# Joining the value products of a head pair into five bursts instead of eight in an attention stage that TensorE shares with its transpositions

## The chip, the cores and the metric

The kernel runs on one core of a Trainium2 chip. The metric is the device time of one execution in microseconds, taken as the median of several runs. The engines are TensorE (PE, with its weight loads PEld), VectorE (DVE), ScalarE (ACT), GpSimd (POOL) and SyncE (SP, which issues DMAs). Each works through its own queue in order and waits on semaphores.

## The reference, cut to what matters

Attention with a mask by hash buckets, for 2 batches of 8 heads, 768 positions and 64 channels, and then two dense layers. The change touches the last line of the attention only, the product of the weights with the values.

```
scores = np.where(mask, scale * q @ k.T, -1e9)
attn = np.exp(scores - scores.max(-1))
attn = attn / (attn.sum(-1) + 1e-9)
out = attn @ v
x = moe(out); return moe2(x)
```

## The kernel before, in words

**Units and pairs.** The heads are taken in eight pairs, numbered here 0 to 7. A pair has 12 units: two heads (`e` 0 and 1) times six blocks of 128 query rows (`i` 0 to 5). A unit goes through four steps on three engines. `QK` on PE (L474, four products of 384 columns) fills a tile `sc` of scores. `MAX` on DVE (L482) reduces it, and `EXP` on ACT (L486) writes `P`. There are two `sc` tiles, so a `QK` waits until the `EXP` of the unit two before it has read its tile.

**Transpositions.** For each block of rows the `P` of both heads, 12 squares of 128x128, is transposed on PE in three pieces `T` of four squares (L509) into a PSUM bank `pt`. ACT copies the bank as the high half in 16 bits (`HI`, L518) and DVE writes the low half (`LO`, L521), both into a tile `PT`. There are two `pt` banks, which the small transpositions `R` of the row factors (L711) use too. So a `T` waits until the `LO` (or the copy of the `R`) two tiles before it has read its bank.

**Value products.** Two blocks of rows make a group of 256 columns, so a pair has three groups, 0 to 2. The products of a group with the values (`PV`, L566) are 36 matmuls of 64 weight columns into one bank `O`, two heads in turn into its lower and upper half. The generator `pv` cuts them into three parts of 12. `EV` on DVE (L575) scales the bank into `xr`. The group's factor comes from `R`, whose source `rb` POOL makes (L725).

**Other steps on PE.** For the next pair PE makes `z` (L398, hash bits) and `xp` (L407, the bits spread over the rows, two pairs of products with a bank of their own).

**The order.** A table `AT` gives each kind of step of a pair a due time, in units of which a pair has 12. Pair `q` adds 12 times `q`. All steps of all pairs are sorted by due time and recorded in that order, and each engine's queue follows from it. The nine due times of `PV` are three for each group. The second and third part of group 0 (9.95 and 10.07) have nothing of PE's between them, so a pair has eight separate bursts. After the attention the queue goes on with the dense layers, where PE is busy throughout.

Of the kernel before, what the change touches and what calls it, by code (L numbers as in the profile page):

```python
# [29 lines left out]
def lsh_attention_glu_act(ctx, tc, qt, kt, v, proj, w_gate, w_val, w_out1, w_in2, w_out2, ident_d, code_d, out):  # L30
# [309 lines left out]
    with ExitStack() as actx:  # L340
# [228 lines left out]
        def evac(b, p, g, O_ps):  # L569
            cs = slice(g * GN, (g + 1) * GN)  # L570
            if g == 0 and p % 2 == 0:
                XX[b, p // 2] = xtile(f"xr_{b}_{p}")
            if g == 0:
                X[b, p] = XX[b, p // 2][:, p % 2]
            nc.vector.scalar_tensor_tensor(out=X[b, p][:, cs], in0=O_ps[:, 0:GN], scalar=1.0 / PSCALE, in1=RS.pop((b, p, g)), op0=ALU.mult, op1=ALU.mult)  # L575
# [9 lines left out]
        with tc.manual_schedule():  # L585
# [109 lines left out]
            def at(kind, i, q, fn, *args):  # L695
                prog.append((UP * q + (AT[kind][i] if isinstance(kind, str) else kind), len(prog), fn, args))

            PP, NQ = {1: p1}, len(seq)
# [41 lines left out]
            for q in range(NQ):  # L740
                us = un[UP * q:UP * q + UP]
                for i, w in enumerate([us[m] for m in (1, 3, 0, 2)] + us[4:] if q == 0 else us):
                    at("QK", i, q, w.QK)
                    at("MAX", i, q, w.MAX)
                    at("EXP", i, q, w.EXP)
                for i in range(PCS * NI):
                    k = i if q else TO[i]
                    x = fl[NI * q + k // PCS]
                    at("T", i, q, x.T, k % PCS)
                    at("HI", i, q, x.HI, k % PCS)  # L750
                    at("LO", i, q, x.LO, k % PCS)
                for i in range(NI // GI):
                    w = us[2 * GI * i + 2 * GI - 1]
                    at((4.3, 7.35, 12.3)[i], 0, q, w.ST)
                    at("ST", i, q, w.ST2)
                    at("RB", i, q, RB, w)
                    at("R", i, q, R, w)
                    at("RS", i, q, RSC, w)
                    for s in range(3):
                        at("PV", 3 * i + s, q, PV, w, s)  # L760
                    at("EV", i, q, lambda w: evac(*w.O), w)
                b, p = seq[q]
                vs = [AT["VR"][0] - UP, AT["VT"][0] - UP, AT["V2"][0], AT["V3"][0], AT["V4"][0]]
                if q == 0:
                    vs[:2] = AT["MAX"][2] + 0.001, AT["MAX"][3] + 0.001
                    at(AT["QK"][3] + 0.001, 0, q, scale_out)
                    at(AT["T"][1] + 0.001, 0, q, scale_in)
                    at(AT["HI"][1] + 0.005, 0, q, scale_keep)
                    vs[2] = max(vs[2], vs[1] + 0.5)
                    vs[3] = max(vs[3], vs[2] + 0.1)  # L770
                    vs[4] = max(vs[4], vs[3] + 0.1)
                elif q == NQ - 1:
                    vs[2:] = (AT["RB"][2] - UP + 0.1 * i + 0.1 for i in range(3))
                for h, d in enumerate(vs):
                    at(d, 0, q, split_v, b, p, h)
                if q + 1 < NQ:
                    at(0.8, 0, q, load_v, *seq[q + 1])
                    if q:
                        at(min(AT["SCL"][0], AT["TOP"][0], AT["TOP"][1]) - 0.01, 0, q, prep, q + 1)
                        at("SCL", 0, q, on, q + 1, "scale")  # L780
                        for j in range(2):
                            at("TOP", j, q, on, q + 1, "top", j)
                            at("RST", j, q, on, q + 1, "rest", j)
                    for i in range(4):
                        at("Z", i, q, on, q + 1, "z", 3 * i, 3 * i + 3)
                        at("XP", i, q, on, q + 1, "xp", *divmod(i, 2))
                        at("H", i, q, on, q + 1, "H", *divmod(i, 2))
                    at("BITS", 0, q, on, q + 1, "bits")
                    at(AT["TOP"][0] + 0.001 if q else -0.9, 0, q, on, q + 1, "copy", 0, 0)
                    at(AT["TOP"][1] + 0.001 if q else -0.65, 0, q, on, q + 1, "copy", 1, 0)  # L790
                    for j in range(2):
                        for m in range(1, 3):
                            at(AT["Z"][3] + 0.01 * m + 0.001 * j, 0, q, on, q + 1, "copy", j, m)
                        at(AT["H"][2 * j + 1] + 0.03, 0, q, on, q + 1, "copy", j, 3)
                        at(AT["H"][3] + 0.035 + 0.005 * j, 0, q, on, q + 1, "copy", j, 4)
                        at(AT["TOP"][j] + 0.002 if q else AT["Z"][3] + 0.03, 0, q, on, q + 1, "copy", j, 5)
                    at(max(AT["H"][3], AT["Z"][3]) + 0.06, 0, q, on, q + 1, "done")
                if q + 2 < NQ:
                    at(0.9, 0, q, load_qk, *seq[q + 2])
            for i in range(12):  # L800
                q, t = ((1, 2.2), (1, 3.4), (1, 4.6), (2, 2.2), (2, 3.4), (2, 4.6), (2, 5.8), (3, 2.2), (3, 4.8), (4, 4.0), (4, 5.0), (4, 6.0))[i]
# [572 lines left out]
```

## Time and profile before

| | before |
|---|---|
| median of 3 runs | 787.75 us (786.75 to 788.44) |
| profiled execution, its own time | 789.26 us |
| span of its instructions | 787.4 us |
| mean granted TensorE clock | 0.997 of full speed |
| PE busy, share of the span | 98% |
| DVE, ACT, POOL busy | 79%, 66%, 21% |

The attention stage takes about the first 250 us. In a timeline row the first number is the start in us from the span's start, the second how long the merged instructions lasted from the first start to the last end, and `x8` how many were merged. The starts of matmuls are recorded. Their ends are modelled and reach beyond the start of the next one, so the distance from one start to the next is what a step occupies PE. Engine `PEld` rows are the weight loads, which run ahead of the products. What stands in square brackets is the idle time before the row, and what ended it.

### The profile page before, as it was taken

What the parts mean: (1) busy time and instruction counts of PE and PEld (TensorE: products, weight loads), DVE (VectorE), ACT (ScalarE), POOL (GpSimd) and SP (SyncE); (2) the same over time, 40 slices, a digit from 0 to 9 for tenths busy, and PEclk for the clock granted to TensorE, in tenths of its full rate; (3) what the DMA queues carried; (4) which work ended last, traced back from release to release, by engine and by line L of the source; (5) the groups of instructions that cost most, each with busy time, mean ns of one, the idle gap of its engine ahead of it and who ended that gap; (6) DMA issues with size and microseconds to landing.
All of it is one profiled execution on the core that took longest, in us unless ns stands there. A gap on an engine that the chain in (4) does not pass through costs nothing.

```text
span 787.4 us, 13055 instructions
## 1 busy us (share of the span) xinstructions
PE 771.5 (98%) x4912; PEld 702.6 (89%) x4912; DVE 624.9 (79%) x1095; ACT 523.1 (66%) x1027; POOL 165.4 (21%) x166
## 2 busy tenths in 40 slices
PE   8999999999989899999999999999999999999997
PEld 5778888888868899999999999999999998898986
DVE  6989988889976878778779959878988867666643
ACT  6988898888865564665664535446766667767653
POOL 4644686783595000000000000000000000000000
PEclk9999999999999999999999999999999999999999
DMA  8845456444101112213212431432333201000002
GB/s 234 198 124 154 100 172 164 105 118 109 34 1 55 54 55 87 75 54 91 72 53 83 133 107 59 147 116 85 104 108 107 82 0 64 18 1 1 0 1 81
DMA packets 41462, 66.98 MB, mean 85 GB/s; under 512 B 5630, under 2 KB 28542, under 8 KB 41398
## 3 DMA queue, kind: packets, MB, share of 16 engines
q1 hardware_dynamic: 40896, 65.82, 28.4%
q8 instruction: 39, 0.64, 0.3%
q10 hardware_dynamic: 502, 0.31, 0.1%
q14 instruction: 25, 0.20, 0.1%
HBM read 45.27 MB, written 3.15 MB: 61 GB/s over the span
## 4 chain that ended last, share of the span: by engine, by line
PE 66%; DVE 1%; ACT 0%; issue 0%; ACTq 0%
PE qa L298 3%; PE qa L296 3%; PE qa L297 3%; PE p L298 3%; PE p L296 3%; PE p L297 3%; PE y L296 2%; PE y L298 2%; PE y L297 2%; PE qe L296 2%; PE qe L298 2%; PE qe L297 2%; PE qb L296 2%; PE qb L298 2%; PE qb L297 2%; PE qa L1134 2%
## 5 line engine op out<-in xcount | busy, mean ns | idle before, releaser
L521 DVE SCALAR_TENSOR_TENSOR PT<-pt,PT 128x512 f16<-128x512 f32 x144 | 96.3, 684 | 16.6 <-ACT PT L518 13.6
L518 ACT ACTIVATE PT<-pt 128x512 f16<-128x512 f32 x144 | 82.4, 597 | 28.8 <-PE pt L509 28.4
L482 DVE TENSOR_REDUCE st<-sc 128x1 f32<-128x768 f32 x96 | 91.0, 949 | 5.3 <-PE sc L474 4.4
L486 ACT ACTIVATE P<-sc,st 128x768 f32<-128x768 f32 x96 | 86.9, 906 | 5.7 <-DVE st L482 5.3
L509 PE MATMUL pt<-ident,P 128*128 128x128 f32 x576 | 79.2, 275 | 2.8 <-DVE PT L521 1.9
L509 PEld LDWEIGHTS pt<-ident,P 128*128 128x128 f32 x576 | 66.1, 140 | 11.7 <-DVE PT L521 6.3
L566 PE MATMUL O<-PT,vh 128*64 128x256 f16 x576 | 54.9, 278 | 0.0
L298 PE MATMUL p<-yh,whl_i 128*128 128x384 f32 x128 | 42.9, 336 | 0.0
L296 PE MATMUL p<-yh,whl_i 128*128 128x384 f32 x128 | 42.9, 335 | 0.0
L297 PE MATMUL p<-yl,whl_i 128*128 128x384 f32 x128 | 42.9, 335 | 0.0
L566 PEld LDWEIGHTS <-vh 128*64 128x64 f16 x576 | 30.7, 109 | 11.2 <-issue 11.2
L1111 ACT ACTIVATE t<-p,cst 128x384 f32<-128x384 f32 x32 | 18.4, 574 | 27.2 <-PE p L298 27.2
L566 PE MATMUL O<-PT,vl 128*64 128x256 f16 x288 | 34.2, 273 | 0.1
L474 PE MATMUL sc<-H,H 128*128 128x384 f32 x96 | 29.6, 390 | 0.8 <-ACT P L486 0.8
L474 PE MATMUL sc<-N,N 128*128 128x384 f32 x96 | 28.9, 382 | 0.3 <-ACT N L412 0.3
L1116 DVE SCALAR_TENSOR_TENSOR gg<-p,t 128x384 f32<-128x384 f32 x32 | 17.7, 555 | 13.3 <-ACT t L1113 13.2
L261 ACT ACTIVATE qb<-qa 128x384 f32<-128x384 f32 x24 | 11.4, 475 | 25.2 <-PE qa L298 14.5
L261 ACT ACTIVATE qd<-qb 128x384 f32<-128x384 f32 x24 | 11.4, 475 | 23.6 <-PE qb L298 20.2
L389 POOL TENSOR_TENSOR W<-n,U 128x768 fp32r<-128x768 f32 x14 | 25.6, 1829 | 0.7
L474 PE MATMUL sc<-U,U 128*128 128x384 f32 x96 | 24.8, 339 | 0.0
L296 PEld LDWEIGHTS p<-yh,whl_i 128*128 128x128 f32 x128 | 24.0, 188 | 0.5
L297 PEld LDWEIGHTS p<-yl,whl_i 128*128 128x128 f32 x128 | 24.0, 188 | 0.5
(1220 smaller groups left out, 2537.0 us busy)
## 6 DMA issues: line engine op xcount, KB each, us to landing
wr_o<-in_moe_w_out_dram SPq DMA_DIRECT2D x28, 512.0 KB, 3.4
H<-U SPq DMA_DIRECT2D x29, 192.0 KB, 3.2
wr_i<-in_moe_w_in_dram SPq DMA_DIRECT2D x8, 512.0 KB, 3.6
wr_i<-in_moe_w_in_dram SPq DMA_DIRECT2D x16, 256.0 KB, 2.9
n<-in_qt_dram SPq DMA_DIRECT2D x8, 384.0 KB, 3.9
n<-in_kt_dram SPq DMA_DIRECT2D x8, 384.0 KB, 4.6
U<-W SPq DMA_DIRECT2D x16, 192.0 KB, 2.6
vr<-in_v_dram SPq DMA_DIRECT2D x8, 384.0 KB, 3.4
```

The lines of the kernel that those rows point to most:

```text
L261: nc.scalar.activation(out=self.new("bcd"[m]), in_=src, func=AF.Copy)
L296: nc.tensor.matmul(ps, lhsT=wh, rhs=rh, start=first, stop=False, **kw)
L297: nc.tensor.matmul(ps, lhsT=wh, rhs=rl, start=False, stop=False, **kw)
L298: nc.tensor.matmul(ps, lhsT=wl, rhs=rh, start=False, stop=last, **kw)
L389: nc.gpsimd.tensor_tensor(out=self.t4[j][1], in0=self.nat[j], in1=f(self.t4[j][0]), op=ALU.subtract)
L474: nc.tensor.matmul(self.sc[:, n, 0:HN], lhsT=M[:, ts], rhs=K[:, n * HN:(n + 1) * HN], start=s0, stop=not s0)
L482: nc.vector.tensor_reduce(out=self.st[:, 0, self.c:self.c + 1], in_=self.sc[:, :, 0:HN], op=ALU.max, axis=AX.XY, negate=True)
L486: nc.scalar.activation(out=self.P, in_=self.sc[:, :, 0:HN], func=AF.Exp, bias=self.st[:, 0, self.c:self.c + 1], scale=1.0, accum_out=self. ...
L509: nc.tensor.transpose(self.ps[m][:, j, :], un[2 * self.n + e].P[:, a, c:c + 128], ident)
L518: nc.scalar.activation(out=self.part(0, m), in_=self.ps[m], func=AF.Copy, scale=PSCALE)
L521: nc.vector.scalar_tensor_tensor(out=self.part(1, m), in0=self.ps[m], scalar=PSCALE, in1=self.part(0, m), op0=ALU.mult, op1=ALU.subtract)
L566: nc.tensor.matmul(O_ps[r, 0:GN], lhsT=vv[m][:, e, i * D:(i + 1) * D], rhs=PT[:, l, e * NI + i, :], start=(s == 0), stop=(s == len(steps) ...
```

## The change

The three parts of a group keep their order and their instructions. Only due times change, and only for pairs 0 to 6. For group 0 all three parts come at the time of the third, 10.07. For groups 1 and 2 the first part comes just ahead of the second, at 12.32 and 17.52. The third parts of these groups (15.54 and 19.68) stay. The last pair keeps its old times.

```diff
                     for s in range(3):
-                        at("PV", 3 * i + s, q, PV, w, s)
+                        k = 3 * i + s
+                        at(AT["PV"][k] if q == NQ - 1 or (i and s) else AT["PV"][3 * i + (2 if i == 0 else 1)] - 0.001 * (2 - s), 0, q, PV, w, s)
                     at("EV", i, q, lambda w: evac(*w.O), w)
```

with the table's row

```
"PV": (8.96, 9.95, 10.07, 11.73, 12.32, 15.54, 16.81, 17.52, 19.68),
```

On DVE, ACT, POOL and SP the same instructions stand in the same order as before. Only PE's queue differs. Group 0 in pair 3 stood on PE like this before. In the names `sc_3_1_4` is pair 3, head 1, block 4 (pairs 4 to 7 are called 0 to 3 again, since the batch's number is left out), `pt` is a transposition bank, `O_3_0` the products of group 0 of pair 3, and `...` stands for the rest of a part.

```order
L474 MATMUL sc_3_1_4_1773<-W_0_3_895,W_0_3_891 128x384 x2
L566 LDWEIGHTS vh_3_1719
L566 MATMUL O_3_0_1778<-PT_3_0_1528,vh_3_1719 64x256
...
L474 MATMUL sc_3_0_5_1813<-H_0_3_896,H_0_3_892 128x384 x2
L474 MATMUL sc_3_0_5_1813<-U_0_3_894,U_0_3_890 128x384 x2
L509 MATMUL pt_0_1819<-ident,P_3_0_4_1752 128x128 x4
L509 MATMUL pt_2_1830<-ident,P_3_1_3_1724 128x128 x4
L566 LDWEIGHTS vh_3_1719
L566 MATMUL O_3_0_1778<-PT_3_0_1528,vh_3_1719 64x256
...
L711 MATMUL r_3_1_3_1861<-ident,rb_3_1_3_1808 128x128 x2
```

The same place in PE's queue now:

```order
L474 MATMUL sc_3_1_4_1773<-W_0_3_882,W_0_3_878 128x384 x2
L474 MATMUL sc_3_0_5_1800<-H_0_3_883,H_0_3_879 128x384 x2
L474 MATMUL sc_3_0_5_1800<-U_0_3_881,U_0_3_877 128x384 x2
L509 MATMUL pt_0_1806<-ident,P_3_0_4_1752 128x128 x4
L509 MATMUL pt_2_1817<-ident,P_3_1_3_1724 128x128 x4
L566 LDWEIGHTS vh_3_1719
L566 MATMUL O_3_0_1824<-PT_3_0_1528,vh_3_1719 64x256
...
L711 MATMUL r_3_1_3_1861<-ident,rb_3_1_3_1795 128x128 x2
```

The first 12 products of the group moved behind one `QK` and two pieces `T`, and all 36 now stand in one row. In group 1 the first 12 move in the same way behind one `QK` of the next pair and two `T`.

Group 2 of pair 3 stood on PE like this before, from the piece `T` ahead of its first part (`sc_0_1_3` belongs to pair 4, `xp` to pair 5):

```order
L509 MATMUL pt_0_2090<-ident,P_0_0_2_2027 128x128 x4
L566 LDWEIGHTS vh_3_1719
L566 MATMUL O_3_2_2095<-PT_3_2_1824,vh_3_1719 64x256
...
L407 MATMUL xp_1_1_1_2113<-bt,code 128x384
L474 MATMUL sc_0_1_3_2118<-N_1_0_1340,N_1_0_1336 128x384 x2
L474 MATMUL sc_0_1_3_2118<-W_1_0_1338,W_1_0_1334 128x384 x2
L509 MATMUL pt_1_2123<-ident,P_0_0_2_2027 128x128 x2
L509 MATMUL pt_1_2123<-ident,P_0_1_2_2079 128x128 x2
L509 MATMUL pt_2_2133<-ident,P_0_1_1_2016 128x128 x4
```

and now:

```order
L509 MATMUL pt_0_2090<-ident,P_0_0_2_2027 128x128 x4
L407 LDWEIGHTS code
L407 MATMUL xp_1_1_1_2100<-bt,code 128x384
L474 MATMUL sc_0_1_3_2105<-N_1_0_1327,N_1_0_1323 128x384 x2
L474 MATMUL sc_0_1_3_2105<-W_1_0_1325,W_1_0_1321 128x384 x2
L509 MATMUL pt_1_2110<-ident,P_0_0_2_2027 128x128 x2
L509 MATMUL pt_1_2110<-ident,P_0_1_2_2079 128x128 x2
L509 MATMUL pt_2_2120<-ident,P_0_1_1_2016 128x128 x4
L566 LDWEIGHTS vh_3_1719
L566 MATMUL O_3_2_2125<-PT_3_2_1811,vh_3_1719 64x256
```

Here the first 12 moved behind one `xp`, one `QK` and two `T`.

## Rows read from the trace of the kernel before

**Rows 1.** Busy time by engine in one stretch: PE, PEld, DVE, ACT, POOL, clock, DMA.

```profile
100.00:140.00 40.00, 39.90 (x349) 33.77 (x349) 35.54 (x57) 35.47 (x75) 29.45 (x31) 1.00 0.58 160
```

**Rows 2.** Waits of PE's products from 20 to 230 us: total, times, longest.

```profile
PE pt L509 <- DVE PT L521: 1.7, 3, 1.1
PE r L711 <- POOL rb L725: 1.2, 1, 1.2
PE r L711 <- DVE PT L521: 0.4, 1, 0.4
PE xp L407 <- ACT bt L401: 0.4, 1, 0.4
```

**Rows 3.** Timeline of PE around group 0 of pair 3.

```profile
115.83 1.03 PE L509 MATMUL pt<-ident,P 128*128 128x128 f32 x8
116.62 0.60 PE L474 MATMUL sc<-N,N 128*128 128x384 f32 x2
...
117.50 0.30 PE L566 MATMUL O<-PT,vh 128*64 128x256 f16 x2
...
118.28 0.62 PE L474 MATMUL sc<-H,H 128*128 128x384 f32 x2
...
119.08 1.04 PE L509 MATMUL pt<-ident,P 128*128 128x128 f32 x8
120.05 0.30 PE L566 MATMUL O<-PT,vh 128*64 128x256 f16 x2
...
120.72 0.82 PE L566 MATMUL O<-PT,vh 128*64 128x256 f16 x12
121.48 0.44 PE L711 MATMUL r<-ident,rb 128*128 128x128 f32 x2
```

**Rows 4.** Timeline of ACT and DVE at the same place.

```profile
117.08 0.90 ACT L486 ACTIVATE P<-sc,st 128x768 f32<-128x768 f32 x1
...
118.60 0.69 DVE L521 SCALAR_TENSOR_TENSOR PT<-pt,PT 128x512 f16<-128x512 f32 x1
```

**Rows 5.** Timeline of PE and DVE around group 1 of pair 3.

```profile
122.45 1.04 PE L509 MATMUL pt<-ident,P 128*128 128x128 f32 x8
...
123.42 0.30 PE L566 MATMUL O<-PT,vh 128*64 128x256 f16 x2
...
123.74 1.29 DVE L521 SCALAR_TENSOR_TENSOR PT<-pt,PT 128x512 f16<-128x512 f32 x2
...
124.20 0.62 PE L474 MATMUL sc<-N,N 128*128 128x384 f32 x2
...
125.02 1.03 PE L509 MATMUL pt<-ident,P 128*128 128x128 f32 x8
```

**Rows 6.** Timeline at group 2 of pairs 2, 3 and 4: low halves and transpositions.

```profile
110.45 0.69 DVE L521 SCALAR_TENSOR_TENSOR PT<-pt,PT 128x512 f16<-128x512 f32 x1 [0.44 <-ACT PT L518]
111.20 0.33 PE L509 MATMUL pt<-ident,P 128*128 128x128 f32 x1
...
111.78 0.30 PE L566 MATMUL O<-PT,vh 128*64 128x256 f16 x2
...
138.27 0.66 DVE L521 SCALAR_TENSOR_TENSOR PT<-pt,PT 128x512 f16<-128x512 f32 x1
138.74 1.04 PE L509 MATMUL pt<-ident,P 128*128 128x128 f32 x8
...
166.16 0.66 DVE L521 SCALAR_TENSOR_TENSOR PT<-pt,PT 128x512 f16<-128x512 f32 x1
166.81 1.03 PE L509 MATMUL pt<-ident,P 128*128 128x128 f32 x8
```

**Rows 7.** Timeline at waits for others, in pair 0 and in pair 7.

```profile
40.85 0.27 DVE L540 TENSOR_REDUCE vrow<-vrow 1x1 f32<-1x129 f32 x1 [1.52 <-DMA vrow<-vm]
...
42.99 0.93 PE L509 MATMUL pt<-ident,P 128*128 128x128 f32 x5 [0.47 <-DVE PT L521]
...
226.86 0.44 PE L711 MATMUL r<-ident,rb 128*128 128x128 f32 x2 [1.21 <-POOL rb L725]
```

## The prediction

> **What bounds the kernel now.** I looked first at the busy time of each engine in a stretch of the attention stage. In 40 us PE is busy for 39.90, DVE for 35.54 and ACT for 35.47 [rows 1]. So PE sets the pace there, and the other two have only about a tenth of their time to spare. Next I read the waits of PE's products from 20 to 230 us: 1.7 + 1.2 + 0.4 + 0.4 = 3.7 us in all, six in number [rows 2]. PE practically never stands. A step that PE loses or gains in a pair therefore moves the end by the same amount, because the dense layers behind the attention are a PE stage too. Last I read the timeline around the three places that the change touches, once for PE, and once for the engines that give PE its tiles back. The reader should see there two things: what a burst costs PE beyond its products, and how long before each `QK` and each `T` its tile had come free.
>
> **What a burst costs.** From the start of two pieces `T` to the start of the `QK` right behind them PE takes 116.62 - 115.83 = 0.79 us [rows 3]. With 12 products between them it takes 124.20 - 122.45 = 1.75 [rows 5]. Inside a longer burst 12 products take 120.72 - 120.05 = 0.67 [rows 3]. So going into a burst and out of it costs 1.75 - 0.79 - 0.67 = 0.29 us. The change removes three bursts in each of seven pairs, 21 in all, which is 21 x 0.29 = 6.1 us of PE's time. That is what could be won. The row thus shows a price for changing between products of 128 and of 64 weight columns. The Trainium skill (TensorEngine Tiling (Array Packing), Key Properties) says why it may be there: changing the tiling mode, and not only the tile, drains TensorE. By that rule alone the change is a gain of these 6.1 us. The trace agrees that the price exists, but not that it is all that changes.
>
> **What the moved steps wait for.** In each of the three places 12 products now stand behind a `QK` and two `T` that they stood ahead of. PE comes to these three about 0.7 to 0.8 us earlier, so their tiles must be free that much earlier. I work it out by the last `T` of each place, since everything that PE does behind it is fixed: two `T` start 0.79 to 0.97 us ahead of what follows them [rows 3], so I put the second one at half of that, 0.44, behind the first. A `T` starts 0.06 us after the `LO` that frees its bank (110.45 + 0.69 = 111.14, and the `T` starts at 111.20) [rows 6]. A second `T` that has not waited is 0.53 ahead of the products (120.05 - 119.52), one that has waited 111.78 - 111.20 = 0.58 [rows 3, 6], so a wait costs 0.05 beside itself.
>
> *Group 0.* Before, the last `T` started at 119.08 + 0.44 = 119.52 [rows 3]. Its bank comes free with the `LO` that ends at 118.60 + 0.69 = 119.29 [rows 4], so it can't start before 119.35. The `QK` ahead of it waits too: PE would be ready for it at 116.62 + 0.80 = 117.42 (a `QK` takes 119.08 - 118.28), but the `EXP` that frees its tile ends at 117.08 + 0.90 = 117.98 [rows 3, 4]. The first products covered this wait, and this cover is gone. Neither the `EXP` nor the `LO` comes sooner in the new order: both work on tiles that PE filled ahead of the place, and their engines' queues are the same. So the `T` moves up by 0.17, and behind it stand 12 products more, 0.67. The end of the burst is late by 0.67 - 0.17 + 0.05 = 0.55 us. `R` at 121.48 comes at 122.03 [rows 3]. Seven pairs: 3.85 us.
>
> *Group 1.* The last `T` started at 125.02 + 0.44 = 125.46. The second of two `LO` ends at 123.74 + 1.29 = 125.03 [rows 5], so it can start at 125.09, 0.37 earlier. Late by 0.67 - 0.37 + 0.05 = 0.35. Seven pairs: 2.45 us.
>
> *Group 2.* Here the pairs differ [rows 6]. In pair 2 (and 1) the last `T` waited for its bank already, so it moves up by nothing: 0.67. In pair 3 (and 0) it started at 139.18 and the bank was free at 138.93: up by 0.19, late by 0.53. In pair 4 (and 5) it started at 167.25, the bank free at 166.82: up by 0.37, late by 0.35. Six pairs: 2 x (0.67 + 0.53 + 0.35) = 3.1 us. In pair 6 the place lies shortly ahead of the `R` at 226.86, for which PE waits 1.21 us on POOL's `rb` [rows 7]. A delay of 0.67 vanishes there: 0.
>
> **What is late next, and what takes a delay up.** Behind each burst PE's queue holds `R` or `xp` and the next `QK`, and for these wait `MAX` on DVE, `EXP` on ACT and then the next `T`. All of them shift by the same delay; PE can't catch up, since it had no waits to give away. The exceptions are waits on something that does not shift. In pair 0 DVE stands 1.52 us for a DMA at 40.85, and PE waits for the `LO` behind it at 42.99, 0.47 before that piece and a little more in the next [rows 7]. The delays of groups 0 and 1 of that pair go into it by some 0.6. The products need no other tile that is late: the bank `O` is evacuated ahead of a group's first part, which comes later now. Instructions that stay in place on the other engines cost nothing, as long as PE is the one that is waited for [rows 1].
>
> **Sum.** 3.85 + 2.45 + 3.1 - 0.6 = 8.8 us longer. The profiled execution's 789.26 becomes 798.1. It stands 1.5 above the median of the runs, so for that I predict 787.75 + 8.8 = **796.5 us**. As a check by PE's own account: idle time of about 2 us in a pair is added (0.6 ahead of the `QK` of group 0, the rest ahead of the `T`), some 15 in all, and 6.1 of switches saved, which leaves about 9.
>
> **The rivals.**
> *Faster: the switches are saved and nothing waits.* For it speaks the 0.29 us of a burst. It would give 787.75 - 6.1 = 781.7. It decides at the last `T`: where its bank is free 0.67 + 0.05 + 0.06 = 0.78 us ahead of its old start, nothing is lost, and with more something is won. The rows show 0.23, 0.43, 0.25, 0.43 and 0.06, so all three places are on the other side, and by 0.35 and more. Only a `LO` that comes much earlier in the new order would bring it, and nothing in the queues lets it. Chance 0.05. The rule of the Trainium skill on tiling modes would by itself give this time.
> *No change.* DVE and ACT, 89% busy, might be what really paces a pair, with PE's steps only filling in; then a lost or saved 0.5 us of PE would drown: 787.75. Against it, PE stands for only 0.1 us in 40 [rows 1]. Chance 0.03.
> *Half of it.* The rest of PE's waits, 3.7 - 0.6 = 3.1 us [rows 2], could take delays up as well, and group 2 could cost 0.35 in all six pairs (1.0 less): 8.8 - 3.1 - 1.0 = 4.7, which is 792.5. Chance 0.08.
> *More.* A burst of 36 products keeps PE for 121.48 - 120.05 + 0.67 = 2.1 us, in which ACT and DVE get no new tile. If they run dry, the `T` behind it come in a heap and wait, say, as long again as those of group 1 now do, 0.4 in each pair: 2.8 more, 799.3. Against it, both have queues that go on with earlier tiles in that time. Chance 0.04.
>
> **How the numbers follow.** The forecast with its own bounds has 0.80. It goes down to 793.4, if PE's other waits take up 3.1, and up to 798.7, if nothing is taken up (0.6 and 0.67 more) and group 2 costs 0.67 in all six pairs (2 x (0.14 + 0.32) = 0.9 more). To leave out no more than 2 in 10 the range takes in the nearer part of the half case: 793.0 to 798.7. A difference of 0.2%, 1.6 us, is about what this kernel's runs can tell from none. Faster 0.05, within it 0.03, slower 0.92, all from the cases above.
>
> **What would show it.** In the profile of the changed kernel PE's wait for `LO` ahead of `T` should be seen at two or three places of every pair, not three times in all, and a new wait of `QK` for `EXP` of about 0.6 us in each of seven pairs. PE's busy time from 100 to 140 us should fall from 39.90 to about 37.5. Products should stand in rows of 36, 24 and 12, with 0.67 for each 12. I am wrong if the `T` ahead of a joined burst start without waiting, or if a pair takes no longer though they wait. Then the `LO` would hang on PE's products in a way that the rows do not show.

## The result, and the profile after

The changed kernel takes 796.25 us (median of five runs, 795.24 to 798.22), the kernel before took 786.75 in the runs beside it. The ratio is 1.012, with a 95% interval of 1.0101 to 1.014, which is 7.9 to 11.0 us longer. The forecast was 8.8 us longer and 796.5 us in all. It counted from 787.75, 1.0 us above the median beside these runs, so part of the close agreement of the totals is luck.

PE's waits come first, since the prediction lives on them. These are the waits of PE's products in the changed kernel from 20 to 235 us: total, times, longest.

```profile
PE pt L509 <- DVE PT L521: 5.0, 14, 1.6
PE sc L474 <- ACT P L486: 4.2, 7, 0.9
PE r L711 <- POOL rb L725: 0.6, 1, 0.6
PE r L711 <- DVE PT L521: 0.4, 1, 0.4
PE xp L407 <- ACT bt L401: 0.3, 1, 0.3
PE xp L407 <- ACT N L412: 0.2, 1, 0.2
```

Before, `T` waited for `LO` three times and no `QK` for an `EXP` [rows 2]. Now it is 14 and 7 times, and the 7 are one in each changed pair. The sum has risen from 3.7 to 10.7 us. The busy time of the stretch that [rows 1] shows has changed with it:

```profile
100.00:140.00 40.00, 38.44 (x336) 32.85 (x333) 33.78 (x54) 33.00 (x69) 27.95 (x29) 1.00 0.57 160
```

PE has lost 1.5 us of its 40. DVE and ACT have lost 1.8 and 2.5, as the same 40 us now hold less of the work. (The view counts a product as busy to its modelled end, so the time from start to start has grown by more.)

Group 0 of pair 3 in the changed kernel, a timeline to lay beside [rows 3, 4]:

```profile
119.71 0.60 PE L474 MATMUL sc<-N,N 128*128 128x384 f32 x2
...
120.17 0.90 ACT L486 ACTIVATE P<-sc,st 128x768 f32<-128x768 f32 x1
...
120.97 0.19 ACT L486 ACTIVATION_READ_ACCUMULATOR P<-sc,st 128x1 f32 x1
...
121.22 0.62 PE L474 MATMUL sc<-H,H 128*128 128x384 f32 x2 [0.56 <-ACT P L486]
...
121.68 0.69 DVE L521 SCALAR_TENSOR_TENSOR PT<-pt,PT 128x512 f16<-128x512 f32 x1
122.04 1.05 PE L509 MATMUL pt<-ident,P 128*128 128x128 f32 x8
...
123.02 0.30 PE L566 MATMUL O<-PT,vh 128*64 128x256 f16 x2
...
124.35 0.82 PE L566 MATMUL O<-PT,vh 128*64 128x256 f16 x12
125.10 0.44 PE L711 MATMUL r<-ident,rb 128*128 128x128 f32 x2
```

The `QK` waits for the `EXP`, as foreseen, and to be exact for the readout of its sum, which ends at 121.16. From the `QK` before it to this one pass 121.22 - 119.71 = 1.51, where PE needs 0.80 for a `QK`. So the wait is 0.71 from start to start, of which the view shows 0.56. The second `T` starts at 122.04 + 0.44 = 122.48, and its bank was free at 121.68 + 0.69 = 122.37. So it did not wait for the `LO`; the `QK` had just held PE up long enough. The 36 products stand in one row, from 123.02 to 125.10, 2.08 us.

Group 1 of the same pair, to lay beside [rows 5]:

```profile
126.08 1.03 PE L509 MATMUL pt<-ident,P 128*128 128x128 f32 x8
...
126.90 0.61 PE L474 MATMUL sc<-N,N 128*128 128x384 f32 x2
...
127.36 1.29 DVE L521 SCALAR_TENSOR_TENSOR PT<-pt,PT 128x512 f16<-128x512 f32 x2
...
128.11 1.25 PE L509 MATMUL pt<-ident,P 128*128 128x128 f32 x8 [0.25 <-DVE PT L521]
...
128.71 0.42 PEld L509 LDWEIGHTS pt<-ident,P 128*128 128x128 f32 x4 [0.18 <-DVE PT L521]
```

Here the `QK` follows the two `T` at once, and both `T` behind it wait for their `LO`; the second for the one that ends at 127.36 + 1.29 = 128.65, and its weights follow at 128.71.

What each place costs is read best from the `R` of the three groups, which stand behind or between the places. Before, the `R` around 121.48 [rows 3] were

```profile
113.87 0.38 PE L711 MATMUL r<-ident,rb 128*128 128x128 f32 x2
...
130.19 0.41 PE L711 MATMUL r<-ident,rb 128*128 128x128 f32 x2
```

and in the changed kernel, around the one at 125.10,

```profile
116.95 0.38 PE L711 MATMUL r<-ident,rb 128*128 128x128 f32 x2
...
134.18 0.41 PE L711 MATMUL r<-ident,rb 128*128 128x128 f32 x2
```

The lag grows from 3.08 over 3.62 to 3.99: group 0 of pair 3 costs 0.54, group 1 costs 0.37. At the end of the attention stage the lag is 7.51 us, or 7.9 counted from the last `R` ahead of the first changed place (which stood 0.40 earlier in this execution). The runs' 9.5 has an interval from 7.9 to 11.0; what it may hold beyond the 7.9 of the attention is not shown by these two traces.

### The profile page after: what moved, and what is told of

It reads as the page before. It is cut to its first block, busy times and chain, and to the rows that moved or that the text cites. A ratio compares the mean times of both kernels' runs of the same rounds, so it can differ in the third digit from the quotient of the medians.

```text
span 793.5 us, 13055 instructions
## 1 busy us (share of the span) xinstructions
PE 770.6 (97%) x4912; PEld 702.4 (89%) x4912; DVE 625.9 (79%) x1095; ACT 524.7 (66%) x1027; POOL 165.2 (21%) x166
## 4 chain that ended last, share of the span: by engine, by line
PE 65%; DVE 1%; ACT 0%; issue 0%; ACTq 0%
PE qa L296 3%; PE qa L297 3%; PE qa L298 3%; PE p L298 3%; PE p L296 3%; PE p L297 3%; PE y L297 2%; PE y L298 2%; PE y L296 2%; PE qe L296 2%; PE qe L297 2%; PE qe L298 2%; PE qb L296 2%; PE qb L298 2%; PE qb L297 2%; PE qa L1135 2%
## 5 line engine op out<-in xcount | busy, mean ns | idle before, releaser
L509 PE MATMUL pt<-ident,P 128*128 128x128 f32 x576 | 81.8, 277 | 6.4 <-DVE PT L521 5.3
L566 PE MATMUL O<-PT,vh 128*64 128x256 f16 x576 | 53.1, 276 | 0.0
```

Source lines behind the costliest of these rows:

```text
L509: nc.tensor.transpose(self.ps[m][:, j, :], un[2 * self.n + e].P[:, a, c:c + 128], ident)
L566: nc.tensor.matmul(O_ps[r, 0:GN], lhsT=vv[m][:, e, i * D:(i + 1) * D], rhs=PT[:, l, e * NI + i, :], start=(s == 0), stop=(s == len(steps) ...
```

## The experiments

Times are medians; ratios are against runs of the kernel before beside them. The diffs are against the kernel before, if not said otherwise.

**One group at a time.** Each of these runs joins one group as the change does.

```diff
-                        at("PV", 3 * i + s, q, PV, w, s)
+                        k = 3 * i + s
+                        at(AT["PV"][k] if q == NQ - 1 or i != 0 or s > 2 else AT["PV"][2] - 0.001 * (2 - s), 0, q, PV, w, s)
```

For group 1 the condition reads `i != 1 or s > 1` and the time `AT["PV"][4]`, for group 2 `i != 2 or s > 1` and `AT["PV"][7]`.

> Only group 0 is joined at the time of its third part. Theory of the tiles (PE reaches the QK and the two T before their tiles are free): about 0.5 us in each of seven pairs, less 0.5 that the wait for a DMA in pair 0 takes up: 3.0 to 3.9 us longer than before. Rival of the long burst (the loss comes from 36 products in a row, which starve ACT and DVE): nearly the whole loss is here, 8 us. Rival of the saved switch alone: 2 us shorter.

> Only group 1's first two parts are joined at the time of the second. Theory of the tiles: 0.35 us in each pair, all of pair 0's taken up by its wait for a DMA: 2.0 to 2.5 us longer. Rival of the long burst: nothing, or 2 us shorter, since the burst has only 24 products. Rival of the saved switch alone: 2 us shorter.

> Only group 2's first two parts are joined at the time of the second. Theory of the tiles: 0.35 to 0.67 us in pairs 0 to 5 and nothing in pair 6, 2.6 to 3.1 us longer. Rival of the long burst: nothing, or 2 us shorter. Rival of the saved switch alone: 2 us shorter.

Group 0 alone: 790.89, ratio 1.0037 (1.0025 to 1.0049), 2.9 us longer. Group 1 alone: 790.77, ratio 1.0029 (1.0016 to 1.0042), 2.3 us. Group 2 alone: 790.59, ratio 1.003 (1.0019 to 1.0042), 2.4 us. The three add up to 7.6, with about 2 to either side, against 9.5 for the whole change. Groups 0 and 2 came out a little under the times expected, within their intervals. PE's waits differ in the way the theory of the tiles says. These rows are the largest of the run of group 0, of group 1 and of group 2, in three views:

```profile
PE sc L474 <- ACT P L486: 4.5, 7, 0.9
```

```profile
PE pt L509 <- DVE PT L521: 2.7, 8, 1.0
```

```profile
PE pt L509 <- DVE PT L521: 3.3, 7, 1.5
```

Group 0 brings the seven waits of `QK` for the `EXP` and no more of `T`, groups 1 and 2 bring waits of `T` for the `LO`. The long burst is not the cause: 36 products in a row are in one of the three runs only, the others cost as much, and in that one `T` waits for `LO` twice, no more often than before. The saved switch alone is refuted by all three.

**The switch by itself.** One more entry into the products, where no `T` and no `QK` moves.

```diff
-                    at("R", i, q, R, w)
+                    at(10.06 if i == 1 and q < NQ - 1 else AT["R"][i], 0, q, R, w)
```

> The order of before, but in pairs 0 to 6 the two transpositions R of group 1 go between the second and the third part of group 0, where nothing stood; behind the third part they stood before. It adds one more entry into products of 64 columns in a pair and moves no T and no QK. If such an entry costs 0.29 us: 2.0 us longer. If the 0.29 read between T and QK is not a price of the switch: no change.

792.56, ratio 1.0054 (1.0039 to 1.0069), 4.3 us longer, twice what was expected. The timeline of PE in pair 3 of this run says why:

```profile
120.60 0.30 PE L566 MATMUL O<-PT,vh 128*64 128x256 f16 x2
...
121.74 0.41 PE L711 MATMUL r<-ident,rb 128*128 128x128 f32 x2 [0.29 <-DVE PT L521]
122.08 0.85 PE L566 MATMUL O<-PT,vh 128*64 128x256 f16 x12
122.85 0.62 PE L474 MATMUL sc<-H,H 128*128 128x384 f32 x2
```

The `R` itself came too early for its bank: 12 products and the way out take 122.85 - 122.08 = 0.77, so it could have started at 121.37 and started at 121.74. This is 0.37 of wait. What is left is 0.77 + 0.34 + 0.77 = 1.88 from the products to the `QK`, against 121.67 - 120.05 = 1.62 before (the `QK` of that place started at 121.67): 0.26 for one more switch. The price read between `T` and `QK` was 0.29. The run was meant to add nothing but a switch and added a wait as well, so it gives the price only through these rows.

**Joined the other way round.** The later parts move up to the first, so the `QK` and the `T` come later in place of earlier. For group 1:

```diff
-                        at("PV", 3 * i + s, q, PV, w, s)
+                        k = 3 * i + s
+                        at(AT["PV"][k] if q == NQ - 1 or i != 1 or s > 1 else AT["PV"][3] + 0.001 * s, 0, q, PV, w, s)
```

> Group 0 joined the other way round: its second and third part move up to the time of the first, so that the QK and the two T come behind all 36 products, 1.3 us later on PE, and one switch in a pair is saved. Theory of the tiles: these three no longer wait, but the EXP and LO that hang on them come about 1 us late, and the QK and T behind the place wait for those: 0.3 to 1.0 us in a pair, 2 to 7 us longer. Rival of the saved switch alone: 2 us shorter.

> Group 1's second part moves up to the time of the first; a QK and two T come 0.65 us later on PE and one switch in a pair is saved. Theory of the tiles: the T and QK behind the place have about as much slack as that, so waits of 0.1 at most are added and a switch of 0.29 is saved: 1.0 to 2.0 us shorter than before, against 2.0 to 2.5 longer when the same parts are joined late. Rival (products in one row cost time wherever they stand): 2 us longer here too.

> Group 2's second part moves up to the time of the first; an xp, a QK and two T come 0.65 us later on PE and one switch of 0.2 to 0.29 us in a pair is saved. Theory of the tiles: the T of the next block comes 0.25 earlier relative to these two and waits about 0.4 for the LO: 0.1 to 0.2 in a pair longer, 0.5 to 1.5 us in all, less than the late join's 2.6 to 3.1. Rival of the saved switch alone: 1.5 to 2 us shorter.

Group 0: 795.21, ratio 1.0094 (1.0077 to 1.0111), 7.4 us longer, just above the 2 to 7 expected. Group 1: 788.82, ratio 1.0009 (0.9995 to 1.0022), no difference that can be measured. Group 2: 790.17, ratio 1.0029 (1.0013 to 1.0044), 2.3 us longer. In the first of the three the wait has moved behind the burst, in all seven pairs, to an `R` whose bank is still being read:

```profile
PE r L711 <- DVE PT L521: 6.8, 7, 1.1
```

For group 1 the 1.0 to 2.0 us expected did not come: the interval reaches no further than 0.4 us shorter. Its trace is shorter by 0.2 at the `R` behind the place in pairs 1 to 5, and in most of them gives 0.1 back until the next place; over the whole stage 0.7 us are won, but 1.0 of gain stands in pair 0 alone, in a stretch where DVE waits for a DMA, so the join itself can't be credited with it. Group 2 costs 0.25 to 0.52 in five of the pairs, and 0.1 to 0.2 were expected.

**Joined in the middle**, behind the `QK` and ahead of the two `T`, for group 1 and, with `17.06` and `i != 2`, for group 2.

```diff
-                        at("PV", 3 * i + s, q, PV, w, s)
+                        k = 3 * i + s
+                        at(AT["PV"][k] if q == NQ - 1 or i != 1 or s > 1 else 12.055 + 0.001 * s, 0, q, PV, w, s)
```

> Group 1's first two parts joined in the middle: behind the QK, which has 1.07 us of slack, and ahead of the two T, which have 0.4 to 0.6. Theory of the tiles: nothing waits that did not, and one switch in a pair is saved: up to 0.29 in each of seven pairs, less what the T behind the place wait because these two come 0.36 later: 0.5 to 2.0 us shorter than before, the best of the joins. Rival (a join costs wherever it stands): 0 to 2 us longer.

> Group 2's first two parts joined in the middle: behind xp and the QK, which has 1.2 to 1.8 us of slack, and ahead of the two T. Theory of the tiles: the two T come 0.4 later than before, and the T behind them waits for their LO as in the early join: between 0.3 longer in a pair (as there) and 0.2 shorter, so from 1.4 us shorter to 2 longer in all.

Group 1: 788.35, ratio 1.0007 (0.9996 to 1.0018), the same as the early join, and not the 0.5 to 2.0 us shorter that were expected. That the `QK` comes later or not makes no difference here. Group 2: 791.61, ratio 1.0045 (1.003 to 1.006), 3.5 us longer and beyond what was expected. Of this, 1.5 us arise at one place in pair 1:

```profile
85.85 1.31 DVE L154 SCALAR_TENSOR_TENSOR wt_g<-wr_g,wt_g 128x512 uint32<-128x512 uint32 x1
...
87.09 0.68 DVE L521 SCALAR_TENSOR_TENSOR PT<-pt,PT 128x512 f16<-128x512 f32 x1
...
87.91 0.41 PE L711 MATMUL r<-ident,rb 128*128 128x128 f32 x2 [1.26 <-DVE PT L521]
```

The `R` waits for a `LO`, and ahead of that `LO` DVE works on weights of the dense layers for 1.31 us, where the same instruction took 0.68 in the kernel before. Why it took longer is not shown. No join is measurably faster than the split order.

**The waits taken away.** If waits for tiles make the loss, a shorter `LO` must take the loss of groups 1 and 2 away and leave the saved switch. This is done in the order of before and in the order of the change.

```diff
-    nc.tensor.matmul(O_ps[r, 0:GN], lhsT=..., rhs=PT[:, l, e * NI + i, :], ...)
+    nc.tensor.matmul(O_ps[r, 0:GN], lhsT=..., rhs=PT[:, 0, e * NI + i, :], ...)
...
-    nc.vector.scalar_tensor_tensor(out=self.part(1, m), in0=self.ps[m], scalar=PSCALE, in1=self.part(0, m), ...)
+    nc.vector.scalar_tensor_tensor(out=self.part(1, m)[:, 0:1], in0=self.ps[m][:, 0:1], scalar=PSCALE, in1=self.part(0, m)[:, 0:1], ...)
```

> The order of before, but DVE writes the low half of the transposed weights for one square of a bank in place of four, and the products with the low half read the high half instead (that part of the sum is wrong, its instructions on PE are the same in number, shape and place). LO becomes about 0.4 us shorter, so the bank of each T is free that much earlier. PE hardly waits before, so theory of the tiles: 0 to 3 us shorter than before. It is the base for the next run.

> The same cut of LO in the order of the change. Theory of the tiles: in groups 1 and 2 the T no longer wait, and each saves its switch, 0.29 and 0.2 in seven pairs, 3.4 us; in group 0 the QK still waits for the EXP, so its 0.4 to 0.5 in a pair stay, 3 us. Together with the cut of LO the change then costs about 0, from 2 us less to 1 us more than the run before it, in place of 8 to 9. Rival (the joined bursts cost by their length or place, whatever DVE does): the full 8 to 9 us stay.

Order of before: 785.87, ratio 0.9971 (0.9957 to 0.9986). Order of the change: 787.77, ratio 0.9998 (0.9986 to 1.001). `LO` takes 0.29 in place of 0.68 us. The change now costs 0.9998 / 0.9971 = 1.0027, 2.1 us with about 1.5 to either side, where it cost 9.5. This is far from the rival's 8 to 9, but its median lies above the 2 less to 1 more that was expected: by the traces less is won in groups 1 and 2 than the 3.4 us counted there. By the starts of `R` group 1 has turned from about 0.35 longer to 0.12 to 0.15 shorter in every pair. Group 2 is 0.20 to 0.23 shorter in pairs 1, 4 and 5, but 0.1 longer in pairs 0 and 3 and 0.49 in pair 2. Group 0 still costs about 0.5, and its wait stands at the head of PE's waits in the second run:

```profile
PE sc L474 <- ACT P L486: 4.6, 7, 0.9
PE pt L509 <- DVE PT L521: 2.3, 2, 1.8
```

**Group 0's wait taken away as well.** Against the run before:

```diff
-    nc.scalar.activation(out=self.P, in_=self.sc[:, :, 0:HN], func=AF.Exp, ...)
+    n = slice(0, 1 if self.e and self.i == 5 else 2)
+    nc.scalar.activation(out=self.P[:, n], in_=self.sc[:, n, 0:HN], func=AF.Exp, ...)
...
     a, c = divmod(i * 128, HN)
+    a = 0 if e and self.i == 5 else a
```

> As the run with the order of the change and the short LO, and besides, the EXP of the one unit in a pair whose tile the QK of group 0 waits for (head 1, block 5) works on half of its columns, so that it ends 0.35 to 0.4 us earlier (its other half of the weights is read from the first half, that part of the result is wrong; PE's instructions keep number, shape and place). Theory that group 0's delay hangs on this EXP and its readout: group 0's step falls from 0.5 us in a pair to 0.1 to 0.2, so 2.1 to 2.8 us shorter than that run, and with the gains of groups 1 and 2 the joined order is then 0 to 1.5 us faster than the split order with the short LO. Rival (36 products in a row cost 0.5 whatever is waited for): no change against that run.

786.83, ratio 0.998 (0.9967 to 0.9993), against the run before 0.998 / 0.9998, 1.4 us shorter. The timeline of pair 3:

```profile
114.48 0.60 PE L474 MATMUL sc<-N,N 128*128 128x384 f32 x2
...
114.94 0.58 ACT L487 ACTIVATE P<-sc,st 128x384 f32<-128x384 f32 x1
...
115.42 0.19 ACT L487 ACTIVATION_READ_ACCUMULATOR P<-sc,st 128x1 f32 x1
...
115.66 0.61 PE L474 MATMUL sc<-H,H 128*128 128x384 f32 x2 [0.24 <-ACT P L487]
```

The `EXP` is 0.32 shorter, and the wait of the `QK` has fallen from 0.56 to 0.24. Group 0's step falls by 0.30 to 0.35 in every pair, to 0.16 to 0.19 in pairs 1, 2, 3, 5 and 6, as the theory had it. What stays is the rest of the same wait: 115.66 - 114.48 - 0.80 = 0.38 from start to start, less the switch. The rival (36 products in a row cost 0.5 whatever is waited for) is refuted by this.

The time falls by less than the 2.1 to 2.8 us expected, though the lag behind group 1 of pair 6 has fallen by 2.5. In this execution 0.46 of that is lost again right there, at group 2 of pair 6: PE waits 1.86 us for a `LO`, and the 24 products behind the wait take 2.70 in place of 1.43 at a lower granted clock.

```profile
220.00:225.00 5.00, 5.00 (x38) 3.95 (x37) 1.69 (x4) 1.58 (x4) 4.92 (x6) 0.66 0.02 5
```

Nine of the twelve runs of this kernel have a mean clock of 0.995, and three of the eleven runs of the one before it. Against the order of before with the short `LO` the joined order is 0.998 / 0.9971, 0.7 us longer, with about 1.5 to either side: the gain of 0 to 1.5 us that was expected is neither shown nor excluded. In the two traces the stage is 0.9 longer. The rest of group 0's wait, group 2 of pair 2 (0.49) and the clock in pair 6 outweigh the switches saved in group 1.

## Why the prediction was right, point by point

**PE sets the pace.** Right. But for the stretch in pair 0 and the wait in pair 4 below, a lag that arises at one of the places is found unchanged at the end of the stage and, but for the clock (last section), at the end of the kernel.

**The price of a switch**, 0.29: an extra one costs 0.26. It was saved 21 times, and with the short `LO` it shows as a gain of 0.12 to 0.23 in all seven places of group 1 and three of group 2. The price depends on the neighbours. In group 0 the burst stood between two `QK`, where PE took 118.28 - 116.62 = 1.66 [rows 3], and without the 0.80 of a `QK` and the 0.67 of the products this leaves 0.19. So the 6.1 us that could be won were put too high, by 0.7 for group 0 alone; the 8.8 does not hang on them. The Trainium skill (TensorEngine Tiling (Array Packing), Key Properties) has the drain at a change of tiling mode. These runs agree that a change costs time, but not by what, and show that it is the smaller part here.

**Group 0**, 0.55 in a pair: measured 0.51 to 0.54 in pairs 1, 2, 3, 5 and 6. The size is right, but the step that led to it is not the one that binds, and that it came out is luck. The prediction put the last `T` at its bank's release. In the trace this `T` doesn't wait, which is one of the prediction's own signs of being wrong. The `QK` ahead of it waits for the readout of the `EXP`'s sum, 0.09 later than the end of the `EXP` that I had used, and then holds PE up to within 0.1 of the same moment. By this wait the place costs 0.71 less the 0.19 of the switch, 0.52. The run with the short `LO` shows it, since there the 0.5 stays, and the run with the short `EXP` takes 0.3 of it away.

**Group 1**, 0.35: measured 0.33 to 0.37 in pairs 1 to 6, by the wait that was foreseen.

**Group 2**, 0.67, 0.53 and 0.35: measured 0.59 and 0.64 in pairs 1 and 2, 0.36 and 0.47 in pairs 0 and 3, 0.33 in pairs 4 and 5, nothing in pair 6. The sum was 3.1 and is 2.7.

**The sum by the trace.** Group 0 gives 3.5 (with 0.66 in pair 0), group 1 in pairs 1 to 6 gives 2.1, group 2 gives 2.7, and the stretch of group 1 in pair 0 takes 0.5 away: 7.9, where the forecast had 8.8. PE's busy time from 100 to 140 us fell to 38.44 and not to 37.5, and the waits in the view grew by 7.0 and not by 15. The view hides a part of each wait behind the modelled ends, and with the switches put too high the forecast of the idle time was too high as well; how much is due to each is not shown.

**What is taken up.** In pair 0 the lag falls by 0.47 from the `R` of group 1 to that of group 2, 0.8 together with the 0.35 that arises there; 0.6 was forecast. This term is not one of the order alone: in the other runs the same stretch gives between 1.0 less and 1.0 more. It holds DVE's wait for the landing of a DMA [rows 7], which lasts 1.86 us in the run of group 1 alone and is absent in the changed kernel. In pair 4 a wait that I had not listed takes up about 0.3 of group 0 (0.24 in place of 0.53). It is found among the waits of weight loads before:

```profile
PEld L566 <- POOL vl L554: 0.2, 1, 0.2
```

Of the rivals, none came. Nothing shows the longer burst to starve anybody: the run of group 0 alone has no more waits of `T` than the kernel before.

## What to carry to other kernels

Where a queue never stands, a step in it may be covering a wait of the next one, and steps that belong together need not be cheaper for standing together. Before moving work behind others, subtract the time when the buffer of each overtaking step came free from its old start: the smallest difference is all by which they can move up, and the length of the moved work is what has to be covered. Do this for all of them and not for the last one alone: in group 0 it was the first that waited. A switch that costs 0.2 to 0.3 us is worth keeping where the work covers a wait of 0.7.

## What the runs showed of the hardware

**The granted clock falls after a long wait in one execution and not in another.** From 258.6 us before, and from 266.1 after, PE waits 2.3 us for the same `qd`. The windows in which the wait ends, before and after:

```profile
260.00:265.00 5.00, 4.13 (x15) 4.16 (x16) 4.23 (x8) 2.98 (x7) 0.00 (x0) 0.66 0.01 3
```

```profile
265.00:270.00 5.00, 2.74 (x16) 2.45 (x15) 4.46 (x9) 3.39 (x7) 0.00 (x0) 1.00 0.01 3
```

Before, the mean granted clock of the window is 0.66, so part of it ran at the lower level of 1.2 GHz; after, it stays at the full 2.4. The lag of the changed kernel falls there from 7.51 to 6.06 us, so the span of the two profiles differs by 6.1 us only, less than the runs do. In the run of group 2 alone the same happens in pair 6: after waits of 0.27 and 1.53 us the 24 products ran at 0.52, and the place cost 0.83, where the changed kernel, after a wait of 1.55 us at the same place, kept its clock and lost nothing (the two windows):

```profile
225.00:228.10 3.10, 3.10 (x29) 2.10 (x27) 1.79 (x3) 1.48 (x3) 3.02 (x3) 0.52 0.02 5
```

```profile
231.00:234.00 3.00, 2.78 (x33) 2.31 (x32) 1.99 (x4) 1.67 (x4) 2.92 (x4) 1.00 0.02 5
```

The five runs of the changed kernel have mean clocks of 0.995 to 1.0 and spread over 3 us, the one at 1.0 is the shortest and the one at 0.995 the longest.

**A tile that an `EXP` with a sum reads is released by the readout of the sum**, 0.09 us after the instruction itself ends (121.16 against 121.07), and the `QK` starts 0.06 behind that. With the short `EXP` the readout ends at 115.42 + 0.19 = 115.61, and the `QK` starts at 115.66.
